# One transpose of x moved from DMA to TensorE, and three key copies moved behind the complex products, in a fused attention and phase-mixing kernel

## The chip, the cores and the metric

The kernel runs on one core of a Trainium2 chip. The metric is the device time of one execution in microseconds (us), as the median over runs. The core has five engines that run at the same time, each through its own list of instructions in order: TensorE (PE in the profile; its weight loads are PEld), VectorE (DVE), ScalarE (ACT), GpSimd (POOL) and SyncE (SP). SyncE only issues DMAs here, GpSimd nearly so. Matmuls write to PSUM, from which VectorE and ScalarE read.

## The reference

Local attention with a few global keys, and on its output a layer that mixes tokens by phases. There are 4 batches, 8 heads, 768 tokens and a head dimension of 64. A query sees the 96 latest keys up to its own position and the first 8 keys.

```
scores = q @ k.T / 8 - slope[h] * dist        # only for k in the last 96 or k < 8
a      = softmax(scores)
x      = concat_heads(a @ v)                  # 768 x 512 per batch
theta  = x @ w_theta
y      = w_tok_r @ (x * cos(theta)) + w_tok_i @ (x * sin(theta))
u      = x + y
out    = u + relu(u @ w_ch)
```

## The kernel before

**Tiles.** A batch has 6 tiles of 128 tokens (index t or tt) and 4 pairs of heads (index p; two heads of 64 fill 128 partitions). Data for the matmuls is bf16.

**Attention of one batch.** For a pair, `qT` and `kT` hold queries and keys with the head dimension on the partitions. `kG` is a second copy of the keys of tiles 1 to 4 in which the first 8 columns of each tile are replaced by the 8 global keys (`kglob`, L221; the wide copy is L227, the one of 8 columns L229). Scores are made in three chunks c per pair, each for two key tiles (`score_mms`, L303: `kT` for the tile's own queries, `kG` for those of the next tile, from the second tile on). ScalarE takes the exponential (L313), VectorE multiplies it by a table of the bias and the mask (L322, L325). `values` (L346) multiplies by v (L362) and divides by the row sum (L371, L373), which writes `x_sb` for the pair. `xtrans` (L375) then makes `xT`, x with the features on the partitions. For batch 0 that is six TensorE transposes into PSUM (L384) and a copy (L385); for batches 1 to 3 it is one DMA transpose that SyncE issues (L377). `xT` has one buffer, `x_sb` two.

**Where q and k come from.** GpSimd issues the loads from memory. For batches 0 to 2 TensorE turns q and k (L253, with copies L257 on VectorE and L259 on ScalarE). For batch 3 they are loaded in token order and turned by DMA transposes from SyncE (`prep_dma`, L264, issued at L270, first the keys and then the queries of a pair). Pair 0 of batch 3 is issued within the attention of batch 2, pairs 1 to 3 just before batch 2's phase products. The second half of batch 3's q and k, and its v, are loaded behind a gate (`load_behind`, L479): GpSimd copies one element of `xT` of batch 1's pair 3 (L480) and issues the nine loads after it.

**The mixing of one batch.** `theta` (L390) multiplies `xT` by `w_theta` (L405) for two token tiles at a time, summing over the four pairs, which are its four blocks of features; three such groups c make the batch. `sines` (L410) takes the cosine and the sine on ScalarE (L415, for the last group in 4 halves) into `cs`, which has two buffers, and VectorE multiplies them by x (L419) into `zri`, the complex products. `mix` (L424) sums the token products for one tile tt over three steps g (L430), and VectorE adds x to give `u` (L435). `utrans` turns u: by DMA from SyncE (L444), or on TensorE with a ScalarE copy (L448, L449). `chan` (L451) multiplies by `w_ch` (L458), and VectorE finishes with relu and sum (L463), which frees the PSUM bank; SyncE writes the result (L465).

**Order.** The first batch's attention is written out by hand. From there on a scheduler orders each engine's instructions by the program's order and its own estimates of costs. In each round of the loop at L624, for batch b, the last channel products of the batch before and all of batch b's `theta` are emitted first (`order`, L631), and then `weave` (L514) puts the steps of the next batch's attention (`attention_steps`, L485) between the steps of batch b's `mix`, `utrans` and `chan`. The scheduler keeps to fences besides: `behind(name)` (L193) says that what is emitted under it is issued, on its engine, after the instruction last stored in `anchor[name]`. `anchor["dve"]` is the latest `u` (L435), `anchor["sp"]` the latest transposing DMA, `anchor["pe"]` the latest token product. Batch 3's key copies stand behind `anchor["dve"]`:

```
        with behind("dve") if b == B - 1 else nullcontext():
            copy(
                out=kG, in_=kT[:, (t0 + 1) * T:(t1 + 1) * T].rearrange("p (t n) -> p t n", t=t1 - t0))
            copy(out=kG[:, :, 0:NG], in_=kT[:, None, 0:NG].to_broadcast([T, t1 - t0, NG]))
```

PSUM has 8 banks: two double banks (`pb`: scores, values, the first two groups of `theta`) and four single ones (`ps`: transposes, token products, channel products, the last group of `theta`).

Of the kernel before, what the change touches and what calls it, by code (L numbers as in the profile page):

```python
# [16 lines left out]
def kernel(  # L17
# [13 lines left out]
    nc = tc.nc  # L31
    B, H, S, D = q.shape
# [4 lines left out]
    NP = H // 2  # L37
# [18 lines left out]
    def ps_small(shape, dtype):  # L56
        return small.tile(shape, dtype, name="ps", tag="ps")
# [129 lines left out]
    anchor = {}  # L187
# [5 lines left out]
    def behind(eng):  # L193

        return tc.issue_after(anchor[eng]) if eng in anchor else nullcontext()
# [25 lines left out]
    def kglob(b, p, t0=0, t1=NT - 2, copy=nc.vector.tensor_copy):  # L221
        kT = qkT[(b, p)][1]
        if t0 == 0:
            qkT[(b, p)][2] = att.tile([T, NT - 2, T], BF, name="kG", bufs=6)
        kG = qkT[(b, p)][2][:, t0:t1]
        with behind("dve") if b == B - 1 else nullcontext():
            copy(  # L227
                out=kG, in_=kT[:, (t0 + 1) * T:(t1 + 1) * T].rearrange("p (t n) -> p t n", t=t1 - t0))
            copy(out=kG[:, :, 0:NG], in_=kT[:, None, 0:NG].to_broadcast([T, t1 - t0, NG]))  # L229
# [11 lines left out]
    def prep(b, p):  # L241
        if p == 0 or (b, p) == (2, NP // 2):
            prep_copy(b, p)
        if p + 1 < NP and (b, p) != (2, NP // 2 - 1):
            prep_copy(b, p + 1)
        qkn = qkns[b, p]
        qT = att.tile([T, S], BF, name="qT", bufs=6)
        kT = att.tile([T, S], BF, name="kT", bufs=6)
        for i_, dst in ((0, qT), (1, kT)):
            ps = ps_small([T, NT, T], BF)  # L250
            with behind("pe"):
                for t_ in range(NT):
                    nc.tensor.transpose(ps[:, t_, :], qkn[:, t_, i_].rearrange("p h d -> p (h d)"), ident)  # L253
            dst = dst.rearrange("p (n t) -> p n t", t=NT)
            src = ps.rearrange("p t n -> p n t")
            if i_ == 0:
                nc.vector.tensor_copy(out=dst, in_=src)  # L257
            else:
                nc.scalar.copy(out=dst, in_=src)  # L259

        qkT[(b, p)] = [qT, kT, None]
        kglob(b, p)
# [66 lines left out]
    def scores(b, p, c):  # L329
        score_mms(b, p, c)  # L330
        score_exp(b, p, c)
# [14 lines left out]
    def values(b, p, hh, i0=0, i1=NT):  # L346
        vn = loads[b][1]
        e_t, vG = ebuf[(b, p)], vGs[b]
        h = 2 * p + hh
        if b == 0:  # L350
            po = ps_small([T, 1, 512], FP)
        else:
            if hh == 0:
                pos[(b, p)] = ps_big()
            po = pos[(b, p)][:, hh:hh + 1, :]
        for it in range(i0, i1):
            mms = [(e_t[:, hh, it, 0, :], vn[:, h, it, :])]
            if it:
                mms.append((e_t[:, hh, it - 1, 1, :], vG[:, h, it - 2, :] if it > 1 else vn[:, h, 0, :]))
            o = po[:, 0, (it - i0) * (D + 1):(it - i0 + 1) * (D + 1)]  # L360
            for i_, (l_, r_) in enumerate(mms):
                nc.tensor.matmul(o, lhsT=l_, rhs=r_, start=(i_ == 0), stop=(i_ == len(mms) - 1))  # L362
        if b and hh == 0:
            return
        if b:
            po = pos[(b, p)]
        h0, n = (hh, 1) if b == 0 else (0, 2)
        nt = i1 - i0
        po4 = po[:, :, 0:nt * (D + 1)].rearrange("p a (t d) -> p a t d", d=D + 1)
        rec = att.tile([T, n, NT, 1], FP, name="rec", tag=f"rec{n}")[:, :, 0:nt]  # L370
        nc.vector.reciprocal(rec, po4[:, :, :, D:D + 1])  # L371
        xv = x_sb[b][:, p, i0:i1, h0 * D:(h0 + n) * D].rearrange("p t (a d) -> p a t d", a=n)
        nc.vector.tensor_mul(xv, po4[:, :, :, 0:D], rec.to_broadcast([T, n, nt, D]))  # L373

    def xtrans(b, p, copy=nc.vector.tensor_copy, i0=0, i1=NT):  # L375
        if b:
            anchor["sp"] = nc.sync.dma_start_transpose(  # L377
                out=xT_sb[b][:, p, :].rearrange("p (t s) -> p t s", t=NT),
                in_=x_sb[b][:, p].rearrange("p t d -> p (t d)")).ins
            return  # L380
        ps = ps_small([T, S], BF)
        own = slice(i0 * T, i1 * T)
        for st in range(i0, i1):
            nc.tensor.transpose(ps[:, st * T:(st + 1) * T], x_sb[b][:, p, st, :], ident)  # L384
        copy(out=xT_sb[b][:, p, own], in_=ps[:, own])  # L385


    zri, u_sb, uTs, pss, css = {}, {}, {}, {}, {}
# [21 lines left out]
    def sines(b, c):  # L410
        pb, xb, last = pss["th", c], x_sb[b], c == NT // 2 - 1
        cs = moe.tile([T, 2, 2, DM], BF, name="cs")
        for i_, bias in ((0, {"bias": halfpi}), (1, {})):
            for o, p_ in [(cs[:, i_, j_], pb[j_]) for j_ in range(2)] if last else [(cs[:, i_], pb)]:
                nc.scalar.activation(o, p_, AF.Sin, **bias)  # L415
        n = 2 if b else 1
        for i_ in range(2):
            for j_ in range(0, 2, n):
                nc.vector.tensor_mul(  # L419
                    zri[b][:, i_, 2 * c + j_:2 * c + j_ + n, :].rearrange("p j (g d) -> p j g d", g=NP),  # L420
                    xb[:, :, 2 * c + j_:2 * c + j_ + n, :].rearrange("p g j d -> p j g d"),
                    cs[:, i_, j_:j_ + n].rearrange("p j (g d) -> p j g d", g=NP))

    def mix(b, tt, g):  # L424
        if g == 0:
# [59 lines left out]
    def attention_steps(b, preps):  # L485

        steps = []
        add = lambda w, f, *a: steps.append((w, lambda: f(*a)))
        add(0, alloc_x, b)
        late = [lambda p=p: prep(2, p) for p in range(NP // 2, NP)] if b == 2 else []  # L490
        chunks = [(p, c) for p in range(NP) for c in range(NT // 2)]
        ahead = [preps[:1], preps[1:2], preps[2:]] if preps else [[]] * 3
        if b == B - 1:
            add(0, kglob, b, 0)
        for i_ in range(0, len(chunks), 2):
            steps.append((1800, lambda i_=i_: [scores(b, *pc) for pc in chunks[i_:i_ + 2]]))
            if i_ == 0:
                add(0, vglob, b, 0, H)
            if b == B - 1 and i_ in (0, 2, 6):
                add(0, kglob, b, (1, 2, 0, 3)[i_ // 2])  # L500
            if i_ in (0, 2):
                steps.extend((1536, f) for f in late[i_ // 2:i_ // 2 + 1])
            if i_ == 8:
                steps.extend((1536, f) for f in ahead[0])
            for p in [p for p in range(NP) if (i_ // 2, p) in ((2, 0), (3, 1), (5, 2))]:
                add(1600, lambda p=p: [values(b, p, 0), values(b, p, 1)])
                add(800, xtrans, b, p)
        steps.extend((1536, f) for f in ahead[1])
        add(1600, lambda: [values(b, NP - 1, 0), values(b, NP - 1, 1)])
        add(800, xtrans, b, NP - 1)  # L510
        steps.extend((1536, f) for f in ahead[2])
        return steps

# [20 lines left out]
    dve, act = nc.vector.tensor_copy, nc.scalar.copy  # L534
# [26 lines left out]
    for p in range(NP - 1):  # L561
        score_exp(0, p, 1)
        out0(p + 1, 1, act)
        out0(p + 1, 0, dve)
        kglob(0, p + 1)
        score_bias(p, 2)
        score_mms(0, p, 2)
        if p:
            values(0, p - 1, 0)
            values(0, p - 1, 1)  # L570
        score_exp(0, p, 2)
        if p < 2:
            vglob(0, 4 * p, 4)
        score_bias(p + 1, 0)
        score_mms(0, p + 1, 0)
        if p + 2 < NP:
            turn0(p + 2, 1)
            turn0(p + 2, 0)
        score_exp(0, p + 1, 0)
        score_bias(p + 1, 1)  # L580
        score_mms(0, p + 1, 1)
        if p == 1:
            xtrans(0, 0)
    p = NP - 1
# [16 lines left out]
    theta(0, 0, 3)  # L601
    xtrans(0, p, dve, 4, 6)
    sines(0, 0)
    theta(0, 1, 2)
    theta(0, 1, 3)
    theta(0, 2, 2)
    theta(0, 2, 3)
    trans_w(1, dve, True)
    sines(0, 1)
    for g in range(NT // 2):  # L610
        for tt in range(2):
# [12 lines left out]
    for b in range(B):  # L624
# [29 lines left out]
        if b == 0:  # L654
            side[:0] = [(0, lambda: load_all_v(2))]
            side.append((0, lambda: (alloc_qk(3), load_qk_tokens(3, 0, H // 2))))
        side += attention_steps(nxt, ahead) if nxt else []
        weave(main, side, 0.1 if b == 0 else 0.0, 0.9)
        rest = [lambda tt=tt, b=b: chan(b, tt) for tt in range(NT - lag, NT)]
# [46 lines left out]
```

## Time and profile before

| | |
|---|---|
| median of 6 runs | 174.64 us (173.12 to 174.99) |
| the profiled execution's own time | 174.64 us |
| its span, first to last recorded instruction | 172.5 us |
| TensorE's granted clock | 1.0 in all 40 slices |
| DMA | 25.93 MB, mean 150 GB/s |
| DMA transposes of x (L377) | 12, from issue to landing 2.7 / 2.8 / 8.0 us (least, median, most) |
| DMA transposes of batch 3's keys (L270) | 4, from issue to landing 2.8 / 2.8 / 3.7 us |

A line of a timeline gives the start, the duration, the engine, the kernel's line, the operation with what it writes and reads, how many instructions are merged in it and, in brackets, how long the engine had sat idle before it and what ended that. A line of the chain gives the start, the duration and what ran: the chain is followed back from the last instruction, at each step to what released it. A matmul's duration includes its way through the array, so that matmuls overlap: one of 512 columns is shown with some 379 ns, while the next starts 216 ns after it.

The waits by engine that concern the lines of the change, in total us, times and the longest:

| who waited | for whom | us |
|---|---|---|
| ScalarE, sines L415 | TensorE, L405 | 14.5 in 4 |
| GpSimd, gate L480 | DMA transpose of x | 9.8 in 1 |
| VectorE, key copy L227 | DMA transpose of keys | 3.4 in 1 |
| TensorE's weight loads L405 | DMA transpose of x | 2.7 in 4 |
| ScalarE, sines L415 | VectorE, zri L419 | 1.3 in 1 |
| TensorE, L405 | DMA transpose of x | 1.0 in 2 |
| TensorE, token product L430 | VectorE, L463 | 0.7 in 1 |

### The profile page before, as it was taken

To read this page: it belongs to the slowest core of one execution; us is meant where nothing else is said; L and a number is where in the kernel's file an instruction comes from. 1 tells how busy PE (TensorE), PEld (TensorE's weight loads), DVE (VectorE), ACT (ScalarE), POOL (GpSimd) and SP (SyncE) were. 2 spreads that over 40 slices of the span, in tenths; PEclk is the share of its full clock that TensorE was granted. 3 is DMA by queue.
4 is the path that set the end of the run, shared out by engine and by line. 5 is a ranking of instruction groups with operands and counts; after the bars stand their busy time and mean duration, and the time that the engine had idled before them with its cause. 6 is when DMAs were issued, how large, how long until landed. Compare 5 with 4: busy or idle time off the path is not lost.

```text
span 172.5 us, 3707 instructions
## 1 busy us (share of the span) xinstructions
PE 158.8 (92%) x1510; PEld 84.2 (49%) x1534; DVE 125.0 (72%) x267; ACT 100.2 (58%) x128; POOL 37.5 (22%) x45
## 2 busy tenths in 40 slices
PE   7679898999999999799999999989999999999991
PEld 2355464565656456244655464433554644444440
DVE  6637677498999999947888788298876865724442
ACT  4698677997587677189964460869446409500010
POOL 8965238002283120099100000000000000000000
PEclk9999999999999999999999999999999999999999
DMA  4999999999999999999996567979145383323335
GB/s 158 195 174 175 209 209 203 206 207 174 159 204 176 180 141 167 194 84 162 166 134 105 144 152 162 138 144 258 26 84 128 93 156 99 122 43 105 99 91 182
DMA packets 75089, 25.93 MB, mean 150 GB/s; under 512 B 63169, under 2 KB 72129, under 8 KB 75073
## 3 DMA queue, kind: packets, MB, share of 16 engines
q0 software_dynamic: 45680, 12.45, 78.3%
q1 hardware_dynamic: 28976, 12.72, 33.5%
q10 hardware_dynamic: 416, 0.52, 0.9%
q8 instruction: 12, 0.20, 0.5%
q14 instruction: 5, 0.03, 0.1%
HBM read 25.69 MB, written 6.29 MB: 185 GB/s over the span
## 4 chain that ended last, share of the span: by engine, by line
PE 59%; DVE 14%; DMA 9%; ACT 8%; POOL 4%; another core or an unknown queue 3%; issue 2%; DVEq 0%; SPq 0%; POOLq 0%; ACTq 0%
PE ps L430 31%; PE ps L458 8%; DMA vn<-in_v_dram 7%; PE pb L362 5%; PE pb L303 4%; PE pb L405 4%; ACT cs L415 4%; POOL qk L73 3%; DMA kT<-qk 2%; DVE qT L257 2%; PE ps L405 2%; PE ps L253 2%; ACT e L313 2%; PE pbw L171 1%
## 5 line engine op out<-in xcount | busy, mean ns | idle before, releaser
L430 PE MATMUL ps<-zri,w_tokT 128*128 128x512 bf16 x273 | 68.0, 379 | 1.6 <-DVE o_sb L463 0.7
L313 ACT ACTIVATE e<-pb 128x1024 bf16<-128x1024 f32 (+1 forms) x48 | 43.7, 954 | 19.3 <-PE pb L303 18.7
L430 PEld LDWEIGHTS <-w_tokT 128*128 128x128 bf16 x288 | 25.9, 98 | 28.8 <-issue 1.2
L435 DVE TENSOR_TENSOR u<-x_sb,ps 128x512 bf16<-128x512 bf16 x24 | 16.3, 680 | 11.6 <-PE ps L430 11.5
L458 PE MATMUL ps<-w_ch_bf,uT 128*128 128x512 bf16 (+1 forms) x97 | 24.2, 371 | 0.4 <-ACT uT L449 0.2
L419 DVE TENSOR_TENSOR zri<-x_sb,cs 128x1024 bf16<-128x1024 bf16 (+1 forms) x30 | 16.4, 579 | 5.5 <-ACT cs L415 5.5
L415 ACT ACTIVATE cs<-pb,halfpi 128x1024 bf16<-128x1024 f32 x8 | 8.9, 1116 | 19.1 <-PE pb L405 14.5
L463 DVE SCALAR_TENSOR_TENSOR o_sb<-ps,u 128x512 f32<-128x512 f32 (+1 forms) x25 | 16.4, 663 | 3.9 <-PE ps L458 3.9
L303 PE MATMUL pb<-qT,kT 64*128 64x128 bf16 x224 | 15.6, 219 | 2.6 <-DVE qT L218 1.4
L303 PEld LDWEIGHTS <-kT 64*128 64x128 bf16 x224 | 9.0, 94 | 15.5 <-issue 13.1
L322 DVE TENSOR_TENSOR e<-e,etab 128x1024 bf16<-128x1024 bf16 (+1 forms) x24 | 14.8, 618 | 2.2 <-ACT e L313 2.2
L405 PE MATMUL pb<-w_theta_bf,xT 128*128 128x512 bf16 x61 | 15.1, 380 | 1.4 <-DMA xT<-x_sb 1.0
L449 ACT COPY uT<-ps 128x512 bf16<-128x512 bf16 x7 | 4.2, 593 | 19.3 <-PE ps L448 19.2
L362 PEld LDWEIGHTS <-e 128*128 128x128 bf16 x352 | 12.9, 97 | 4.9 <-issue 2.5
L405 PEld LDWEIGHTS <-xT 128*128 128x128 bf16 x96 | 8.8, 98 | 12.5 <-DMA xT<-x_sb 2.7
L458 PEld LDWEIGHTS <-uT 128*128 128x128 bf16 x100 | 9.1, 98 | 9.8 <-ACT uT L449 0.7
L88 POOL DMA_DIRECT2D vn<-in_v_dram x5 | 9.6, 1916 | 14.3 <-DVE qkn L238 12.6
L303 PE MATMUL pb<-qT,kG 64*128 64x128 bf16 x128 | 11.6, 217 | 0.6 <-DVE kG L229 0.4
L373 DVE TENSOR_TENSOR x_sb<-pb,rec 128x768 bf16<-128x768 f32 x12 | 11.4, 953 | 0.3
L362 PE MATMUL pb<-vn,e 128*128 128x65 bf16 x168 | 9.7, 193 | 0.5 <-DVE x_sb L373 0.3
L325 DVE TENSOR_TENSOR e<-e,etab 128x1024 bf16<-128x1024 bf16 x12 | 8.2, 687 | 2.5 <-ACT e L313 2.4
L259 ACT COPY kT<-ps 128x768 bf16<-128x768 bf16 x8 | 6.4, 798 | 4.6 <-PE ps L253 4.4
(75 smaller groups left out, 201.6 us busy)
## 6 DMA issues: line engine op xcount, KB each, us to landing
out_dram<-o_sb SPq DMA_DIRECT2D x23, 256.0 KB, 2.4
vn<-in_v_dram POOLq DMA_DIRECT2D x3, 768.0 KB, 20.2
qk<-in_q_dram POOLq DMA_DIRECT2D x2, 768.0 KB, 21.1
qk<-in_k_dram POOLq DMA_DIRECT2D x2, 768.0 KB, 24.0
w_nat<-in_moe_w_tok_r_dram POOLq DMA_DIRECT2D x3, 384.0 KB, 15.8
w_nat<-in_moe_w_tok_i_dram POOLq DMA_DIRECT2D x3, 384.0 KB, 15.1
vn<-in_v_dram POOLq DMA_DIRECT2D x2, 384.0 KB, 10.2
qk<-in_q_dram POOLq DMA_DIRECT2D x8, 96.0 KB, 8.9
```

The source lines that it names most:

```text
L303: nc.tensor.matmul(pb[:, hh, o:o + T], lhsT=lhsT, rhs=qT[R, (own, nxt)[part]], start=bool(b), stop=bool(b) or (jt == NT - 1 or (j == 1 and ...
L313: ins = nc.scalar.activation(e_c, pb[:, :, 0:n], AF.Exp, scale=scale).ins
L322: nc.vector.tensor_mul(e_c, e_c, tab[:, :, s0:s0 + n // T].rearrange("p a s n -> p a (s n)"))
L362: nc.tensor.matmul(o, lhsT=l_, rhs=r_, start=(i_ == 0), stop=(i_ == len(mms) - 1))
L373: nc.vector.tensor_mul(xv, po4[:, :, :, 0:D], rec.to_broadcast([T, n, nt, D]))
L405: nc.tensor.matmul(pb[j_] if last else pb[:, j_, :], lhsT=xT[:, dc, st(j_)], rhs=w_theta_bf[:, dc, :], start=(dc == 0), stop=(dc == NC - 1))
L415: nc.scalar.activation(o, p_, AF.Sin, **bias)
L419: nc.vector.tensor_mul(zri[b][:, i_, 2 * c + j_:2 * c + j_ + n, :].rearrange("p j (g d) -> p j g d", g=NP), xb[:, :, 2 * c + j_:2 * c + j_ ...
L430: anchor["pe"] = nc.tensor.matmul(ps, lhsT=w_tokT[wi][:, st, tt * T:(tt + 1) * T], rhs=zri[b][:, wi, st, :], start=(st == 0 and wi == 0), ...
L435: anchor["dve"] = nc.vector.tensor_add(u_sb[b, tt].rearrange("p (g d) -> p g d", g=NP), x_sb[b][:, :, tt, :], ps.rearrange("p (g d) -> p g ...
L458: nc.tensor.matmul(ps_c, lhsT=uT[:, dc, :], rhs=w_ch_bf[:, dc, i_ * n:(i_ + 1) * n], start=(dc == 0), stop=(dc == NC - 1))
L463: nc.vector.scalar_tensor_tensor(o_sb[:, cols], in0=ps_c, scalar=0.0, in1=u[:, cols], op0=ALU.max, op1=ALU.add)
```

## The change

Two things change. First, `xtrans` takes the TensorE path for pair 3 of batch 1 also: six transposes (L384) and a copy to `xT` (L385), with ScalarE as the copying engine; the DMA transpose of that pair goes. The pairs 0 to 2 of batch 1 and all of batches 2 and 3 are turned by DMA as before, and the copying engine that is passed for them is not used. The gate copy on GpSimd reads the same element of `xT`, which ScalarE now writes.

Second, each zri product is stored in a new anchor, and batch 3's key copies of pairs 1 to 3 are issued on VectorE behind the latest zri, which is the last one of batch 2, in place of the latest u. Pair 0's copies stay where they were. What is computed is the same.

```
     def kglob(...):
...
-        with behind("dve") if b == B - 1 else nullcontext():
+        with behind("zri" if p else "dve") if b == B - 1 else nullcontext():
...
     def xtrans(b, p, copy=nc.vector.tensor_copy, i0=0, i1=NT):
-        if b:
+        if b > 1 or (b and p < 3):
             anchor["sp"] = nc.sync.dma_start_transpose(
...
     def sines(b, c):
...
-                nc.vector.tensor_mul(
+                anchor["zri"] = nc.vector.tensor_mul(
                     zri[b][:, i_, 2 * c + j_:2 * c + j_ + n, :].rearrange("p j (g d) -> p j g d", g=NP),
                     xb[:, :, 2 * c + j_:2 * c + j_ + n, :].rearrange("p g j d -> p j g d"),
-                    cs[:, i_, j_:j_ + n].rearrange("p j (g d) -> p j g d", g=NP))
+                    cs[:, i_, j_:j_ + n].rearrange("p j (g d) -> p j g d", g=NP)).ins
...
     def attention_steps(b, preps):
...
-                add(800, xtrans, b, p)
+                add(800, xtrans, b, p, nc.scalar.copy)
...
-        add(800, xtrans, b, NP - 1)
+        add(800, xtrans, b, NP - 1, nc.scalar.copy)
```

## The prediction

> **What bounds the kernel now.** I read the page's busy times first, then the windows by stage, then the timeline of each engine around the two places that the change touches, and last the chain of work that ended last.
>
> ```profile
> span 172.5 us, 3707 instructions
> PE 158.8 (92%) x1510; PEld 84.2 (49%) x1534; DVE 125.0 (72%) x267; ACT 100.2 (58%) x128; POOL 37.5 (22%) x45
> ```
> ```profile
> 70.00:80.00 10.00, 8.80 (x44) 3.67 (x44) 7.26 (x15) 5.95 (x9) 6.53 (x9) 1.00 1.15 134
> 80.00:106.00 26.00, 25.74 (x276) 14.05 (x280) 21.16 (x38) 15.65 (x19) 2.42 (x2) 1.00 1.31 145
> 106.00:118.00 12.00, 11.21 (x62) 4.83 (x63) 7.89 (x17) 8.26 (x10) 0.00 (x0) 1.00 0.85 155
> 118.00:140.00 22.00, 21.53 (x229) 11.41 (x233) 17.46 (x32) 11.38 (x14) 0.00 (x0) 1.00 0.49 115
> ```
>
> The windows give the stretch, its length, then the busy time of PE, PEld, DVE, ACT and POOL. TensorE is the bound: 25.74 of 26.00 us from 80 to 106 and 21.53 of 22.00 us from 118 to 140. The two stretches in which a new batch starts leave a hole: 1.20 us of TensorE idle from 70 to 80 and 0.79 us from 106 to 118. Whatever closes a hole moves all behind it forward, since TensorE waits for almost nothing between and after them.
>
> The first hole, TensorE's timeline at the start of batch 1's phase products:
>
> ```profile
> 70.39 0.59 PE L405 MATMUL pb<-w_theta_bf,xT 128*128 128x512 bf16 x2
> 71.78 1.47 PE L405 MATMUL pb<-w_theta_bf,xT 128*128 128x512 bf16 x6 [0.79 <-DMA xT<-x_sb]
> 73.40 1.90 PE L405 MATMUL pb<-w_theta_bf,xT 128*128 128x512 bf16 x7 [0.16 <-DMA xT<-x_sb]
> ```
>
> It waits twice on transposes made by DMA: until 71.78 for pair 2 (issued by SyncE at 68.01) and until 73.40 for pair 3 (issued at 70.52, landed 2.9 us later). A 512-wide matmul takes its turn in 0.216 us (eight in 1.73).
>
> The second hole, the chain between batch 2's phase products and batch 3's first scores:
>
> ```profile
> 108.22 3.75 DMA kT<-qk
> ...
> 111.99 0.29 DVE kG L227
> ...
> 112.97 0.61 DVE zri L419
> ...
> 113.65 2.24 ACT cs L415 x4
> ...
> 115.91 1.28 ACT L313
> ...
> 117.21 1.03 ACT e L313
> ...
> 118.28 0.34 PE pb L303 x6
> ```
>
> VectorE stands at the copy of pair 1's keys until a transposed load lands, and behind it in VectorE's queue stand the complex products (zri), whose cosines were ready. ScalarE's last sines then wait for the zri that frees their buffer, and the exponentials wait for the sines.
>
> **Part 1: pair 3 of batch 1 on TensorE.** Removed: one SyncE transpose (1.24 us of SyncE's time, with its landing). Added: six 128x128 transposes, one ScalarE copy. TensorE's order, read from the changed program, becomes: eight token products (L430), two L405, six transposes, four u transposes, four channel products, then the rest of L405. From 67.57: eight products 1.73, to 69.30; two L405, to 69.73; then x of pair 3, which VectorE finishes at 70.00 (L373, 69.03 for 0.97), so a wait to 70.05; six transposes in 0.34 (the chain's row for six L384), to 70.39; u 0.22, to 70.61; channel products 0.86, to 71.47; and the wait for pair 2 to 71.78 as before. All the additions fit in the old hole, with 0.31 us to spare; without that cover they would cost 0.34 us. The ScalarE copy takes 0.80 us by the nearest row (L259, same 128x768 from PSUM), 70.6 to 71.4, where ScalarE stood idle from 69.45 to 74.05, and two matmuls ahead of its first reader at least.
>
> From 71.78 six L405 end at 73.08 and the seventh finds its data: 0.32 us saved. The first cosine, 0.43 us behind the last matmul of its group before (73.62 to 74.05), starts at 73.29 instead of 74.05: 0.76 earlier, and so do the ScalarE steps that follow. TensorE: eight L405 to 74.81, u to 75.03, eight to 76.76, channel products to 77.62. The next channel products wait for uT: its copy moves from 77.86 to 77.10, they follow 0.67 us after (as 78.53 before), at 77.77, and end at 78.64. The first token product of batch 1 starts there (79.40 before); the VectorE step that frees its bank (L463, ended 79.32) moves by the same 0.76, so it does not bind. Three score matmuls that ran before this point now run behind it, 0.17 us. Net: **0.59 us**. Bounds: nothing gained and 0.34 lost if the transposes were exposed; 0.76 if the exponentials' shift carried alone.
>
> One DMA price is not in the trace: pair 2's landing beside a different neighbour. It took 3.76 us; transposes took 2.7 to 8.0. At 2.8 it would land at 70.8 and give 0.31 more; I keep 3.76, because its issue time and all queued before it stay. GpSimd's gate copy (73.41) waits for ScalarE's copy now, so its nine queued loads for batch 3 start some 1.8 us earlier. Their first user in SyncE's queue stands at 98.56, so this is worth nothing, and pair 2 has landed when they start.
>
> The trace's six L384 took 0.34 us together (219 ns each, overlapped), and that row is used. A rule speaks against it: the Trainium skill, "VectorE: DVE Perf Modes", section "The three transpose paths", prices a 128x128 transpose on TensorE at 390 ns. Six would be an estimated 2.34 us, 2.0 more than the row, of which 0.31 is covered; part 1 would then lose 1.1 us and the whole sum would come to 174.6.
>
> **Part 2: the key copies of batch 3.** Three pairs of copies (0.29 and 0.17 us each) move behind the last zri; nothing is added, and the orders of TensorE, ScalarE, GpSimd and SyncE stay there. On the old time axis: first zri at 109.54 (cosine 108.41 for 1.11), the second at 110.47, ended 111.15 instead of 113.56; the channel output L463 at 111.2 to 111.8 instead of 113.48 to 114.16. TensorE waited 0.66 us for that L463 (114.21); now its token products follow its channel products at 113.40. ScalarE's last sines need only TensorE's sums: the last but one L405 group ends near 112.54, so the four sines run 112.54 to 114.78 (2.24 as in the chain), the table load to 116.07, the first exponential to 117.11, and TensorE's next scores start at 117.17 instead of 118.28: **1.11 us**. TensorE has that much to give up: 0.81 to 114.21, 0.29 within L430 at 117.22 (for the last zri), 0.26 at 118.28, together 1.36, which is the upper bound; zero is the lower one.
>
> What is late next: the copies themselves. The last zri ends near 115.5, two key copies take it to 116.1, and pair 3's keys, issued as here:
>
> ```profile
> 114.09 1.23 SPq L270 DMA_TRANSPOSE kT<-qk  x1
> ```
>
> land 2.8 us later (the kT rows: 2.8, 2.8, 3.7), at 116.9. VectorE waits 0.8 us there. Behind it are u (L435) and the three bias multiplications of batch 3's first pair; with the steps of before (0.6, 0.7, 0.7, 0.56) they end at 119.96. Their reader, TensorE's values (122.12, now 121.0), has 1.0 us in hand. Pair 1's keys are needed at 119.31, now 118.2, and are copied by 116.5.
>
> **Sum.** 0.59 + 1.11 = 1.70 us off the span: 172.5 to 170.8. The profiled run took 174.64, 2.14 above its span and equal to the median of the six runs, so 170.8 + 2.14 = **172.9 us** (−1.0%).
>
> **The rivals.** (B) Part 1 moves its wait and gains nothing: ScalarE, which now has the x copy and two uT copies around the cosines, or pair 2's landing, holds TensorE to its old time. For it: TensorE still waits at 71.78, and two steps (uT, L463) bind the token products within 0.1 us. Against it: ScalarE's idle 4.6 us. Time 174.64 − 1.11 = 173.5. (C) Part 2 gains nothing: the copies in a row take back what the zri gave, because pair 3's keys come 1.1 us past the slack. Time 174.64 − 0.59 = 174.05. (D) Neither counts, or run-to-run drift hides it: 174.6. (E) Slower: VectorE is held at pair 3's key copy. It costs from a landing 3.8 us after issue (114.09 + 3.8 + 0.1 = the 1.0 us of slack used up), eats both gains at 5.5 us, and decides from there. The worst transpose of the page, 8.0 us, would give 174.64 + 2.5 = 177.1. Against it: that 8.0 fell where the DMA share was 2.11, while 106 to 118 has 0.85 and its key transposes took 2.8 to 3.7. That the change does not do what it says is excluded by the changed program's order, which shows both moves.
>
> **How the numbers follow.** Forecast 0.62, B 0.13, C 0.11, D 0.06, E 0.08. About 0.5% (0.87 us) is what a measurement of this kernel can tell from no change; the six runs spread from 173.12 to 174.99. Faster means under 173.77: all but 0.05 of the forecast and two thirds of B (0.09), 0.66. Slower: E, 0.08. The rest, 0.26, is within. Range: the upper bounds 0.76 and 1.36 give 172.5, and 0.4 for the spread of runs gives 172.1; on the other side B, C and part of D belong in, to 174.5. What is left out is E and the edges, under 2 in 10.
>
> **What would show it.** Right: the wait at 73.40 is gone and the first cosine stands near 73.3; TensorE's waits in 70 to 80 total about 0.7 us instead of 1.2; no wait for L463 near 113; the table load after batch 2's sines ends 1.7 us earlier on the clock; a key copy waits on its DMA for about 0.8 us with no wait of L362 behind it. Wrong: a landing of pair 2 later than 71.8, token products of batch 1 at 79.4 again, or a TensorE wait on a bias multiplication at the first values of batch 3.

## The result and the profile after

| | before | after |
|---|---|---|
| median | 173.83 us (66 runs) | 172.83 us (29 runs) |
| span of the profiled execution | 172.5 us | 170.3 us |

The ratio after to before is 0.9944, with a 95% interval of 0.9929 to 0.9959: 0.97 us less (0.71 to 1.23). The predicted 172.9 us is met, but not for the right reason. The sum of 1.70 us was taken from the 174.64 us of the first six runs, whose median lies 0.81 us above that of all 66; of the 1.70 us a little more than half came. Two later profiled executions, one of the kernel after and one of a variant, ran far longer than the rest (206.96 and 890.08 us), and their traces are not read here.

The span and the engines' busy times from the page of after, and below them its windows by stage, in the same columns as those of before:

```profile
span 170.3 us, 3718 instructions
PE 158.5 (93%) x1516; PEld 84.3 (49%) x1540; DVE 125.7 (74%) x267; ACT 100.9 (59%) x129; POOL 37.8 (22%) x45
```
```profile
70.00:80.00 10.00, 9.79 (x61) 4.40 (x61) 8.42 (x15) 8.72 (x12) 9.28 (x10) 1.00 1.39 151
80.00:105.00 25.00, 24.79 (x263) 13.57 (x266) 20.24 (x36) 14.04 (x17) 0.12 (x1) 1.00 1.25 136
105.00:117.00 12.00, 11.36 (x69) 4.96 (x68) 9.31 (x21) 9.44 (x12) 0.00 (x0) 1.00 0.80 171
117.00:139.00 22.00, 21.79 (x226) 11.50 (x230) 16.55 (x29) 10.20 (x12) 0.00 (x0) 1.00 0.50 114
```

The first hole has shrunk from 1.20 to 0.21 us of idle TensorE. The second still has 0.64 us, after 0.79. TensorE's timeline in the first hole, and ScalarE's:

```profile
68.56 0.59 PE L405 MATMUL pb<-w_theta_bf,xT 128*128 128x512 bf16 x2
69.32 0.51 PE L384 MATMUL ps<-ident,x_sb 128*128 128x128 bf16 x6 [0.16 <-DVE x_sb L373]
69.66 0.39 PE L448 MATMUL ps<-ident,u 128*128 128x128 bf16 x4
69.89 1.03 PE L458 MATMUL ps<-w_ch_bf,uT 128*128 128x512 bf16 x4
70.91 3.20 PE L405 MATMUL pb<-w_theta_bf,xT 128*128 128x512 bf16 x13
```
```profile
69.86 0.80 ACT L385 COPY xT<-ps 128x768 bf16<-128x768 bf16 x1 [2.82 <-PE ps L384]
70.56 0.59 ACT L449 COPY uT<-ps 128x512 bf16<-128x512 bf16 x1
72.42 1.11 ACT L415 ACTIVATE cs<-pb,halfpi 128x1024 bf16<-128x1024 f32 x1 [1.27 <-PE pb L405]
```

The transposes follow x, the copy of 0.80 us falls into ScalarE's idle time, and L405 runs on from 70.91 without the waits of before. Only part of the earlier clock is the change's: this execution stood 0.74 us ahead before TensorE's changed order began (the token products at 66.83, 67.57 before). It was already ahead by 1.08 us at the first L405 of the kernel (25.44, 26.52 before), up to which the instructions of the two kernels are the same. So stretches between fixed points are compared below, not times of day.

The chain of waits through the second hole, after:

```profile
103.37 3.32 DMA xT<-x_sb
106.69 0.05 issue
106.73 2.33 PE pb L405 x10
...
111.48 2.24 ACT cs L415 x4
...
113.73 1.28 ACT L313
...
115.03 1.03 ACT e L313
...
116.10 0.34 PE pb L303 x6
```

The key copy is gone from the chain. In its place, ahead of the hole, stands a transpose that did not limit so long before: that of batch 2's pair 3. SyncE's issue of it took 1.79 us in place of 1.24, first before, then after:

```profile
104.94 1.24 SPq L377 DMA_TRANSPOSE xT<-x_sb  x1
```
```profile
103.37 1.79 SPq L377 DMA_TRANSPOSE xT<-x_sb  x1
```

It landed 3.32 us after its issue began, in place of 2.8.

### The profile page after: what moved, and what is told of

It reads as the page before. It is cut to its first block, busy times and chain, and to the rows that moved or that the text cites. A ratio compares the mean times of both kernels' runs of the same rounds, so it can differ in the third digit from the quotient of the medians.

```text
span 170.3 us, 3718 instructions
## 1 busy us (share of the span) xinstructions
PE 158.5 (93%) x1516; PEld 84.3 (49%) x1540; DVE 125.7 (74%) x267; ACT 100.9 (59%) x129; POOL 37.8 (22%) x45
## 4 chain that ended last, share of the span: by engine, by line
PE 61%; DVE 17%; DMA 10%; POOL 5%; ACT 3%; issue 1%; DVEq 0%; POOLq 0%
PE ps L430 30%; PE ps L458 9%; DMA w_nat<-in_moe_w_tok_i_dram 8%; PE pb L405 7%; PE ps L405 4%; PE pb L303 4%; PE pb L362 3%; DVE qT L257 3%; POOL qk L73 3%; DVE x_sb L373 2%; DVE e L322 2%; DMA xT<-x_sb 2%; POOL vn L88 2%; DVE e L325 1%; DVE o_sb L463 1%
## 5 line engine op out<-in xcount | busy, mean ns | idle before, releaser
L463 DVE SCALAR_TENSOR_TENSOR o_sb<-ps,u 128x512 f32<-128x512 f32 (+1 forms) x25 | 16.4, 663 | 4.1 <-PE ps L458 3.6
L405 PE MATMUL pb<-w_theta_bf,xT 128*128 128x512 bf16 x61 | 15.0, 379 | 0.8 <-DMA xT<-x_sb 0.4
L405 PEld LDWEIGHTS <-xT 128*128 128x128 bf16 x96 | 9.0, 98 | 11.7 <-DMA xT<-x_sb 1.8
```

Of the source, the lines that this page charges most:

```text
L405: nc.tensor.matmul(pb[j_] if last else pb[:, j_, :], lhsT=xT[:, dc, st(j_)], rhs=w_theta_bf[:, dc, :], start=(dc == 0), stop=(dc == NC - 1))
L463: nc.vector.scalar_tensor_tensor(o_sb[:, cols], in0=ps_c, scalar=0.0, in1=u[:, cols], op0=ALU.max, op1=ALU.add)
```

## The experiments

**How they are compared.** Behind the token products at which TensorE's order begins to change, five stretches are read from TensorE's timeline of each trace, from start to start: hole 1, to the first L253 after batch 1's first token products; then to batch 2's first L405 (24.70 or 24.71 us in every kernel but one); "x wait", to the channel products after the first 16 L405 (traces lack a few matmul records, so that some show only 15 of them); hole 2, to the third chunk of batch 3's first scores; the rest, to the last u transpose (48.43 to 48.59). Only three move:

| kernel | ratio of the run (95%) | hole 1 | x wait | hole 2 | all five |
|---|---|---|---|---|---|
| before, first trace | | 14.16 | 3.50 | 8.34 | 99.21 |
| before, again | 0.9972 (0.9949 to 0.9996) | 14.66 | 3.48 | 7.81 | 99.25 |
| part 1 alone | 0.9935 (0.9916 to 0.9954) | 13.36 | 4.14 | 7.40 | 98.03 |
| part 2 alone | 0.9936 (0.9910 to 0.9963) | 14.78 | 3.50 | 7.20 | 98.68 |
| after, first trace | 0.9944 (0.9929 to 0.9959) | 13.33 | 4.04 | 7.20 | 97.71 |
| after, third | 0.9953 (0.9932 to 0.9975) | 13.91 | 4.27 | 7.20 | 98.56 |
| after, 12 places earlier | 0.9941 (0.9917 to 0.9965) | 13.94 | 3.47 | 7.20 | 97.75 |
| before, 12 places later | 1.0061 (1.0040 to 1.0082) | 14.75 | 5.18 | 7.20 | 100.27 |
| part 1 alone, 12 places earlier | 1.0006 (0.9986 to 1.0025) | 14.53 | 3.48 | 8.42 | 99.64 |
| after, 40 places later | 0.9933 (0.9908 to 0.9959) | 13.81 | 4.34 | 7.20 | 98.48 |
| after, 72 places later | 0.9934 (0.9912 to 0.9956) | 13.75 | 3.67 | 7.20 | 97.76 |
| after, and batch 2's pair 3 on TensorE | 0.9928 (0.9901 to 0.9954) | 13.38 | 3.45 | 7.20 | 97.50 |

Before against itself gave 0.9972, so a ratio can be 0.3% off, and ratios are best held against those of kernels measured together. "Places" are places in TensorE's list of instructions, counted in matmuls and weight loads.

**Do the parts add?** Each part was run alone, beside both together and the kernel before.

```
part 1 alone:  xtrans as in the change; kglob and sines as before
part 2 alone:  kglob and sines as in the change;  xtrans:  if b:
```

> Only part 1: pair 3 of batch 1 on TensorE, the key copies where they were. Theory A (the two parts add, as predicted): 0.59 us off, ratio 0.9966. Theory B (part 1's gain is given back at batch 2's phase products, where the DMA transpose of pair 3 landed 3.3 us after issue in the trace of after and 2.8 in that of before): 0.0 to 0.2 us off, ratio 0.999 to 1.000, and TensorE waits again 0.4 us or more at L405 near 107. Theory C (part 1 is worth what the two traces show between the first token product of batch 0's last tile and batch 1's, 0.83 us): ratio 0.9952.

> Only part 2: the key copies of pairs 1 to 3 behind the last complex product, x by DMA as before. Theory A: 1.11 us off, ratio 0.9936; the first scores after the second hole 1.1 us after where the part alone would put them, no wait for L463. Theory D (the chain through the key copy stood that late only in the one profiled execution, and in most others the transposed keys land earlier): 0.3 to 0.7 us off, ratio 0.996 to 0.998.

> Both parts, once more, on the chip of the two single ones. If the parts add, the ratio is the product of theirs. Theory A: 0.990; by the runs so far 0.9944 with 0.9929 to 0.9959. The second trace tells whether the 1.79 us issue and 3.3 us landing of batch 2's pair 3 belong to the kernel (then they stand here too, theory B) or to the execution (then 1.2 and 2.8).

> The kernel before as a second trace. Theory D says that the wait of VectorE at pair 1's keys is shorter than 3.4 us here, or that issue at 109.55 takes 1.23 and not 1.78 us; theory A that the wait is 3.0 to 3.5 us again.

They do not add. Part 1 alone gave 0.9935, part 2 alone 0.9936 and both, measured together with them, 0.9935 (0.9911 to 0.9959); against the second run of before, which was measured with them too, each of the three is at 0.996. So part 1 alone was worth no less than theory A gave it and more than B did, and part 2 alone about what A gave it, but both together are worth no more than one. The table tells why. Part 1 takes 0.8 to 1.4 us out of hole 1. But with it the x wait grows from 3.50 to 4.14 us, which is theory B's mechanism, though not its price (TensorE waits 0.51 us at L405 at 107.39), and hole 2 falls to 7.40 without part 2: the first of the later pairs of keys lands 2.80 us after its issue there, and 3.75 before. Of hole 2, part 2 then has only 0.20 us left to take. The long transpose stands in the trace of part 1 (issue 1.87 us, landing 3.42) as in that of after and in the third of after (1.98 and 3.55), so it goes with part 1. Theory D holds in small: the second trace of before has a hole of 7.81, not 8.34, and VectorE waits 2.87 us, not 3.43.

**What moves the long transpose?** DMA traffic from 102 to 106 us, in 40 slices of 0.1 us, first before, then after:

```profile
DMA  8259899896100005999999995100399999720000
GB/s 170 49 164 307 307 369 430 328 451 226 41 0 0 0 3 118 215 225 215 220 205 220 210 208 106 23 0 0 49 195 220 218 218 205 174 34 0 0 0 0
```
```profile
DMA  9999999972061789999990000000100289999999
GB/s 202 218 218 228 205 218 202 200 147 39 15 166 36 138 182 205 233 189 174 65 8 8 8 10 10 10 10 10 16 0 0 49 164 195 236 192 215 200 207 218
...
q8 instruction: 1, 0.02, 1.5%
```

After has something that before lacks there: a packet of the queue that the page calls instruction (q8, 12 packets and 0.20 MB in the whole run). The time given for such a packet is the start of the window, mostly of 0.25 us, in which it was found. Where it falls, at 103.0, the transposes move at some 200 GB/s until 104.0 and then at 8 to 10 GB/s until 104.9, as if one DMA engine of 16 did its share late. Before has such a packet in the microsecond from 109 on, in the keys' transposes:

```profile
q8 instruction: 1, 0.02, 7.2%
```

That is 7.2% of 16 engines, 1.15 us of one. In part 1 alone it stands at 103.75, in part 2 alone at 108.25. It goes with part 1, and part 1 puts six transposes with their weight loads into TensorE's list: 3,080 matmuls and weight loads in place of 3,068 (and one more instruction that only waits for a semaphore). Twelve packets of 16 KB are 256 instructions each if one has 64 bytes, 3,072 in all. So I took the packets for fetches of TensorE's instructions, and theory F says that the added transposes moved one of them. The Trainium skill, "Runtime: NRT & Kernel Launch", section "Instruction fetch mechanics", says the same of the block: 16 KiB, 256 instructions, fetched by the sequencer over a DMA queue of its own. It calls the cost mostly hidden; here it is not, as the next runs show (0.5 to 1.7 us of the x wait).

**Theory F tested: move TensorE's list, and nothing else.** The kernel starts with six matmuls on a zero tile that nobody reads. Leaving them out, or doubling them, moves all later TensorE instructions by 12 places; the lists of the other engines stay as they are.

```
-    warm(6)
+    warm(0)       # 12 places earlier;   warm(12): 12 places later
```

> The changed kernel without the six idle matmuls on a zero tile at its start, so that every later instruction of TensorE stands 12 places earlier in its list, as in the kernel before. Theory F (the six added transposes move an instruction fetch of TensorE from batch 3's keys to batch 2's last x transpose): the fetch near 103 us goes back to some 107 to 109, the transpose issued near 103.5 takes 1.2 us and not 1.8 to 1.9, the stretch from the first L405 of batch 2 to the next channel products is 3.50 us and not 4.04, and the ratio against before goes from 0.9944 to 0.991 or 0.992. Rival G (the slow transpose comes from GpSimd's earlier loads or from the shorter queue of SyncE): the stretch stays at 4.0 to 4.1 and the ratio at 0.9944.

> The kernel before with six more idle matmuls at the start: 12 places later, as behind the added transposes. Theory F: the fetch comes at 103 to 105 us, together with the transpose of pair 3 of batch 2: 4.0 to 4.1 us in that stretch in place of 3.50, and the second hole behind it falls from 7.8 to 8.3 to some 7.4 us, so that the time stays within 0.2% of before. Rival G: 3.50 us and 7.8 to 8.3 us as in before.

> Only part 1, and 12 places earlier. Theory F: 3.50 us in the stretch of batch 2's first L405, and the second hole back at 7.8 to 8.3 us (7.40 in part 1 alone), so that the time is within 0.2% of part 1 alone. Rival G: 4.1 and 7.4.

SyncE's transposes of batch 2's pair 3 and of batch 3's first later pair of keys, in after with 12 places less:

```profile
103.87 1.24 SPq L377 DMA_TRANSPOSE xT<-x_sb  x1
...
107.16 1.95 SPq L270 DMA_TRANSPOSE kT<-qk  x1
```

The long issue has gone from x back to the keys, the fetch stands at 107.5, and the x wait is 3.47 us, as F had it. In before with 12 places more, TensorE's timeline:

```profile
106.87 1.46 PE L405 MATMUL pb<-w_theta_bf,xT 128*128 128x512 bf16 x5
109.88 2.33 PE L405 MATMUL pb<-w_theta_bf,xT 128*128 128x512 bf16 x10 [1.56 <-DMA xT<-x_sb]
```

Here the fetch came at 106.5, the wait for pair 3 became 1.56 us and the stretch 5.18; hole 2, freed of the fetch, fell to 7.20 without part 2. Six idle matmuls at the start made the kernel 0.6% slower, which is twice what before differs from itself; their own time is not the reason, since the token products ahead of hole 1 start no later than before (67.42 us, 67.57 before). I had expected the fetch at 103 to 105 us and the time within 0.2%: the fetch did meet pair 3's transpose, but later, and the collision cost 1.7 us and not 0.6. Rival G is out, since in all three pairs of kernels (after, before and part 1 alone, each at two placements 12 apart) GpSimd's and SyncE's lists were the same on both sides, and the x wait changed.

Two more expectations of F failed. After with 12 places less was not faster (0.9941), because hole 1 grew to 13.94. And part 1 with 12 places less gained nothing at all (1.0006): hole 1 was 14.53.

```profile
69.48 0.38 PE L405 MATMUL pb<-w_theta_bf,xT 128*128 128x512 bf16 x1
71.40 0.39 PE L405 MATMUL pb<-w_theta_bf,xT 128*128 128x512 bf16 x1 [1.55 <-DMA xT<-x_sb]
```

That is part 1 with 12 places less: TensorE waits for pair 1, one of the transposes that were left on DMA. Part 1's order starts L405 ahead of a group of u transposes and one of channel products that stood before it until then, so it needs pairs 0 and 1 some 1.1 us sooner (1.73 us behind the first token product, 2.82 before). In the trace of before, pair 1 landed 1.3 us ahead of its reader, so that little is left; here it was issued at 61.53 and landed 9.8 us later, where the trace of before has 7.9.

These runs also give part 2 its worth in both placements of the fetch. With the fetch on the keys: 174.11 to 173.04 us, 1.07 us, and hole 2 from 8.42 to 7.20 (hole 1 of the two traces differs too, by 0.59 us, so the times alone would not tell). With the fetch on x: 173.09 to 173.10 us, nothing, and 7.40 to 7.20.

**Can the fetch be put where it does no harm?** The six wide idle matmuls became 26 of 128 columns or 42 of 64, so the list moved by 40 or 72 places; after was run a third time beside them.

```
-            nc.tensor.matmul(ps, lhsT=zero[:, 0:T], rhs=zero, start=True, stop=True)
+            nc.tensor.matmul(ps[:, 0:64], lhsT=zero[:, 0:T], rhs=zero[:, 0:64], start=True, stop=True)
...
-    warm(6)
+    warm(42)
```

> The changed kernel with 26 narrow idle matmuls (128 columns) at the start in place of 6 wide ones, so that TensorE's list stands 40 places later. Theory F: the fetch of 103.0 us moves forward by the time of 40 places, to some 102.3, and meets the last x transpose of batch 2 less: the stretch of batch 2's first L405 between 3.5 and 4.0 us, and 0.1 to 0.5 us less than after, ratio 0.991 to 0.994, if the fetch in the first hole does no more harm than now. Rival: 4.0 us and the ratio of after, 0.9944.

> The same with 42 idle matmuls of 64 columns, 72 places later. Theory F: the fetch at some 101.5 us, before the last x transpose of batch 2 is issued: 3.50 us in the stretch, 0.5 us less than after, ratio 0.991, again if the first hole stays at 13.1 us. Rival: 4.0 us and 0.9944.

> The changed kernel once more. From the end of batch 1's values to the last u transpose of TensorE the two kernels before took 99.00 and 99.04 us and the changed one 97.50; if that is its usual time, 97.4 to 97.8 again and a ratio near 0.9914. If the first hole is often worse (a wait for pair 1 or 2 of x, as part 1 with 12 places less had it), 98.0 to 98.5 and a ratio near 0.9944.

With 40 places the fetch came at 102.0, as expected, but the x wait stayed long (4.34): it met the transposes queued before pair 3, which was itself issued only at 104.49. With 72 places it came at 101.25 and the wait fell to 3.67. The fetch in hole 1 moved too, to 66.0, and there pair 1 was late:

```profile
68.85 0.38 PE L405 MATMUL pb<-w_theta_bf,xT 128*128 128x512 bf16 x1
70.00 0.39 PE L405 MATMUL pb<-w_theta_bf,xT 128*128 128x512 bf16 x1 [0.76 <-DMA xT<-x_sb]
```

So with 72 places hole 1 lost (13.75 for 13.33) what the x wait gained (3.67 for 4.04), with 40 both were longer than in the first trace of after, and neither ratio (0.9933, 0.9934) can be told from that of after. The third run of after brought the answer to the question of size: its trace has 98.56 us over the five stretches, against 97.71 in the first (the expectation counts from a point 0.21 us later), with a wait of 0.58 us for pair 2 in hole 1 and 4.27 in the x wait. The gain of 1.50 us between the first two traces was a good case; 99.23 to 98.14, the means of two traces each, is 1.09 us, and the runs say 0.97.

**Pair 3 of batch 2 on TensorE too.**

```
-        if b > 1 or (b and p < 3):
+        if b > 2 or (b and p < 3):
```

> The changed kernel, and pair 3 of batch 2 turned on TensorE with a ScalarE copy too. The wait of L405 near 107 goes whatever makes it long: some 3.46 us in that stretch, with 0.33 us of transposes ahead of it. Theory F and rival G alike: 0.1 to 0.5 us less than after, ratio 0.992 to 0.994; if ScalarE or a bank of PSUM binds instead, 0 or more.

> Pair 3 of batch 2 on TensorE too, for a trace that can be read: 3.46 us in the stretch of batch 2's first L405 with 0.33 us of transposes ahead of it, the first cosine of batch 2 some 0.5 us earlier than in after, ratio 0.990 to 0.994.

The x wait is gone (3.45), for 0.34 us of transposes ahead of it, and the five stretches are the shortest of all, 97.50. The first cosine of batch 2 comes 0.26 us sooner than in after, counted from the end of hole 1, and not 0.5 as expected. The ratios of the two runs, 0.9936 (0.9913 to 0.9958) and 0.9928 (0.9901 to 0.9954), lie at or below that of after, but not clear of it. It is a candidate, not shown to be faster than after.

## Why the prediction was right in its steps and wrong in its sum

**The two holes.** Right as to where TensorE stood idle before: the 24.70 us ahead of the x wait and the 48.5 us behind hole 2 kept their length within 0.2 us in all twelve traces of the table, apart from the 0.34 us of transposes that the last one adds. But the prediction let all gains through because TensorE waits for almost nothing between the holes, and there the change made a wait: the x wait.

**Part 1 in its own hole.** Right in mechanism. The six transposes took 0.34 us, as the trace's row said, and not the 2.34 us that the prediction estimated from the 390 ns of the Trainium skill, "VectorE: DVE Perf Modes", section "The three transpose paths". No wait came up on ScalarE or at L463. Of rival B only the other half came, and in part: a late pair 2 held TensorE in three of the traces with part 1 (by 0.48 to 0.62 us), a late pair 1 in two. The size was too small: 0.59 us forecast, 0.83 between the first two traces (14.16 to 13.33). Of the 0.24 us more, 0.13 is pair 2, which came that much sooner after the token products than the prediction kept it, and the rest is the score matmuls that moved behind, which cost 0.06 us and not 0.17. The wait for pair 3 that part 1 removes was 0.16 us in the profiled execution, but 0.85 to 0.89 in the three other traces in which pair 3 was still on DMA and TensorE waited there; in those three SyncE's issue of pair 2 took 2.4 to 2.5 us and not 1.21, and the issue of pair 3 stood behind it. Against this, hole 1 was longer again when pair 1 or 2 came late, and the prediction kept pair 2's 3.76 us without saying that the new order needs pair 1 sooner. GpSimd's earlier loads did nothing, as forecast: the 24.70 us behind them did not change.

**Part 2.** Right for the profiled execution: 1.11 us forecast, 1.14 measured in hole 2 (8.34 to 7.20). VectorE's queue after, behind the last zri:

```profile
114.36 0.49 DVE L227 COPY kG<-kT 128x512 bf16<-128x512 bf16 x2
114.77 0.17 DVE L229 COPY kG<-kT 128x32 bf16<-128x32 bf16 x1
115.34 0.29 DVE L227 COPY kG<-kT 128x512 bf16<-128x512 bf16 x1 [0.40 <-DMA kT<-qk]
115.54 0.29 DVE L229 COPY kG<-kT 128x32 bf16<-128x32 bf16 x2
115.80 0.69 DVE L435 TENSOR_TENSOR u<-x_sb,ps 128x512 bf16<-128x512 bf16 x1
```

It waited 0.40 us for pair 3's keys (0.8 forecast), and the values did not wait: rivals C and E, which needed late keys, did not happen. In the second trace of before there was less to win: 0.61 us (7.81 to 7.20).

**The step that failed** is the sum, 0.59 + 1.11, and in it the sentence that all of part 1's additions fit in the old hole. Their time does; their places in TensorE's list were not counted. Twelve places moved a fetch of instructions from the keys' transposes to the last x transpose of batch 2. That costs 0.54 us (4.04 for 3.50; 0.77 in the third run), a term that the sum lacked, and it takes away most of the stall that part 2 was to remove: 1.11 us counted, 0.20 left once part 1 is in. By the first two traces the account closes: 0.83 − 0.54 + 1.14 = 1.43 of the 1.50 us that all five stretches lost. By the means of two traces each, before and after, hole 1 gives 0.79, the x wait takes 0.67, hole 2 gives 0.88 and the rest 0.09: 1.09 us, where the runs say 0.97. So hole 1 gave more than the 0.59 forecast and hole 2 less than its 1.11; together they came near the forecast 1.70, and what was left out is the 0.67 of the x wait. That 172.9 us was met all the same is luck: the start of the sum was 0.81 us too high, and the gain too large by nearly as much.

**Still open.** The place in the list that sets off a fetch is not settled. The weight load that waits for batch 2's pair 3 stands at place 2217 before and 2229 after, and a boundary between the two would explain the jump from 103 to 109; but before with 12 places more has the load at 2229 too and its fetch came at 106.5. What makes pairs 1 and 2 late in hole 1, the fetch there (at 66.0 to 69.0 in all traces) or GpSimd's loads beside it, was not separated.

The traces show two things more that no run explains. With part 1, hole 1 is 13.33 to 13.38 us in the three traces in which the fetch fell 0.5 to 0.8 us after the start of SyncE's issue of pair 2, and that issue took 2.4 to 2.5 us; it is 13.75 to 14.53 in the five in which the fetch fell elsewhere and the issue took 1.2 us (the first trace of before has an issue of 1.21 us with the fetch 0.5 us after its start, so this alone does not decide). The length goes with the place of the fetch there too, then, but why a longer issue goes with a pair 2 that lands sooner (3.6 us after its issue began, and 3.9 to 4.2) is not known. And the token products ahead of hole 1 start at 66.57 to 67.25 us in the seven traces with part 2 and at 67.36 to 67.75 in the five without it, although nothing of part 2 runs before them. If this is more than chance, part of the measured gain lies ahead of the five stretches.

## What to carry to other kernels

A gain read from one trace holds for the placement of everything in it: run each part alone before adding the gains. Where transposes by DMA end on the path within a microsecond, instructions added to a list of thousands, as TensorE's here, can move a fetch into them; look for the instruction queue in the DMA view of both traces, and shift the list by a few idle instructions to see what that is worth. And take the wait that an edit removes from several traces: here it was 0.16 us in one and 0.85 to 0.89 in the others.

## What the runs showed that I had not expected

An instruction fetch of 16 KB holds up transposes that SyncE issues: an issue took 1.8 to 2.2 us in most traces where the fetch fell on it, not 1.23, and a landing on the path came 0.5 to 1.7 us late. Six idle matmuls of no use, whose own time is made up long before the first hole, made the kernel 0.6% slower (1.0061, 1.0040 to 1.0082).
